# Gate and up as pairs of 64-row matmuls on two row tiles

## The chip, the cores and the metric

The kernel runs on one core of a Trainium2 chip. The metric is the device time of one execution in microseconds. A program that is run again differs by some tenths of a per cent; the three runs of the kernel before lie between 1452.52 and 1454.48 us.

## The reference

The kernel computes one block over 2048 tokens of width 576: a layer norm, a linear attention `s`, a gated feed-forward part, and a product of both.

```python
xn = _layernorm(x)                       # x: 2048 x 576
s = _A_ref(xn, A_wqkv, A_wo)             # linear attention, 32 heads of 18
g = xn @ B_w_gate                        # 576 x 4608
u = xn @ B_w_up                          # 576 x 4608
h = _gelu(g) * u
return x + s * _silu(h @ B_w_down)       # 4608 x 576
```

All operands are fp32. The matrices of gate, up and down are the bulk of the work.

## The kernel before

TensorE works through five stages: `kv` and `q` (projections of the normalized x), `s` (the attention's output, kept in DRAM), gate and up, and down. The change lies in gate and up, with small edits where their operands are formed.

**Words.** A matmul on fp32r operands keeps part of the mantissa. So every operand is split into a high part (a copy by ScalarE that rounds, `act(..., AF.Copy)`) and the remainder (a subtraction by VectorE), and a product is taken in several passes: high by high, high by remainder, remainder by high.

**Seven products for eight.** A gate or up matrix of one group `g` (256 columns of 4608) is multiplied by a scheme of Strassen's kind (`matrix`, from L916): K is split into two halves of 288, the 256 columns into two blocks of 128, and the tokens into blocks of 512. Seven products in place of eight give four output blocks. On the side of the weights GpSimd forms the sums S1 to S4 (`mat_sums`), on the side of x VectorE formed T1 to T4 once (`difference`, L337). The seven products write PSUM banks al, be, ga, de; three of them add to a bank that is begun already:

| product | bank | weights, x |
|---|---|---|
| 0 | al | A11, B11 |
| 1 | be | S2, T2 |
| 2 | ga | S1, T1 |
| 3 | de | S3, T3 |
| 4 | al, added | A12, B21 |
| 5 | ga, added | S4, B22 |
| 6 | de, added | A22, T4 |

Each is done for two sides of the tokens, s = 1 and then s = 0 (tiles named `xo_` and `xr_`, the latter read back from DRAM by `back`). There are 18 groups, gate and up by turns: 36 matrices, `q` from 0 to 35.

**Passes.** A half of K has 288 = 128 + 128 + 32 rows. The operand tiles hold five blocks for it: high parts 0 and 1, a mixed block 2 in which the last 32 rows stand several times as high parts and remainders, and remainders 3 and 4. `product` (L907) runs the seven passes of `PASSES`, each a matmul of 128 rows, 128 columns of weights and 512 tokens.

**What follows a product** is written behind it in `matrix`: copies and sums of the banks by ScalarE and VectorE, gelu and the multiplication in `done`, and the pieces of `todo`: the cutting of the next matrix's weights into words (`mat_pieces`, `cut_w`), the load of the matrix after (`load_mat`), and `run_events`, which issues the sums over h (GpSimd) and their stores to DRAM (SP's queue). The order on every engine is the order of the program. There are six banks for be, ga and de, two of their own for al.

**Down** begins behind matrix 35. `down_first` puts its first loads and cuts into that matrix's `todo`: `load_reg("22")` and `load_reg("42")` (weights of down into the places of B11 and T2 of side 0, `REG` and `X_BACK` both 13 and 7), `load_unit(0, ...)` (tiles `raw_a`, `raw_b` from DRAM) and `cut`. They go through SP's queue, in that order. The bd matmuls need `hi` (ScalarE) and the remainder in `raw_a` (VectorE).

Lines in the profile: L147 is the helper `mm`, L141 `act`, L144 `vec`, L150 `pool`, L153 `dma`; L909 is the matmul in `product`.

## Time and profile before

| | |
|---|---|
| median of three runs | 1453.16 us |
| the profiled execution | 1452.58 us |
| its span on the core | 1450.9 us |
| instructions | 22169 |
| granted clock of TensorE | 1.00 |

The profile is one execution. PE is TensorE's matmuls, PEld its loads of weights, DVE VectorE, ACT ScalarE, POOL GpSimd, SP the engine that issues most DMAs. A group reads: line, engine, operation, names (out<-in), shape, count | busy us, mean ns of one | idle us before, and who ended it. `128*128` is the rows and columns of the array in use. A row of a stretch gives, engine by engine, the busy us with the count in brackets, then the granted clock, the share of the DMA engines and GB/s. A row of the timeline gives start, duration, engine, line, operation, names, shape and count, and in square brackets the idle time before it. A row of waits gives who waited for whom: total us, times, longest.

### The profile page before, as it was taken

What the parts mean: (1) busy time and instruction counts of PE and PEld (TensorE: products, weight loads), DVE (VectorE), ACT (ScalarE), POOL (GpSimd) and SP (SyncE); (2) the same over time, 40 slices, a digit from 0 to 9 for tenths busy, and PEclk for the clock granted to TensorE, in tenths of its full rate; (3) what the DMA queues carried; (4) which work ended last, traced back from release to release, by engine and by line L of the source; (5) the groups of instructions that cost most, each with busy time, mean ns of one, the idle gap of its engine ahead of it and who ended that gap; (6) DMA issues with size and microseconds to landing.
All of it is one profiled execution on the core that took longest, in us unless ns stands there. A gap on an engine that the chain in (4) does not pass through costs nothing.

```text
span 1450.9 us, 22169 instructions
## 1 busy us (share of the span) xinstructions
PE 1444.4 (100%) x8272; PEld 1286.5 (89%) x8272; DVE 1148.7 (79%) x1609; ACT 565.2 (39%) x918; POOL 580.1 (40%) x520
## 2 busy tenths in 40 slices
PE   9999999999999999999999999999999999999998
PEld 8989989988888888888888888888889999999998
DVE  7688666476787887887777878778888978989898
ACT  6444365333222233322332232332235556555454
POOL 3342340225756567566475754667632000000000
PEclk9999999999999999999999999999999999999999
DMA  5554115521532315224242243323379888767886
GB/s 221 186 205 158 45 36 207 224 95 51 171 101 100 131 52 188 88 95 140 72 159 87 97 150 102 117 87 121 126 272 347 269 261 252 249 188 235 278 293 225
DMA packets 119253, 235.04 MB, mean 162 GB/s; under 512 B 11658, under 2 KB 45354, under 8 KB 117226
## 3 DMA queue, kind: packets, MB, share of 16 engines
q1 hardware_dynamic: 116346, 221.37, 45.4%
q0 software_dynamic: 2656, 12.06, 2.2%
q8 instruction: 65, 1.06, 0.3%
q14 instruction: 42, 0.34, 0.1%
q10 hardware_dynamic: 144, 0.20, 0.0%
HBM read 150.96 MB, written 82.58 MB: 161 GB/s over the span
## 4 chain that ended last, share of the span: by engine, by line
PE 97%; DVE 1%; ACT 1%; issue 0%; POOL 0%; DVEq 0%; ACTq 0%; POOLq 0%
PE bd L147 25%; PE al L909 16%; PE ga L909 16%; PE de L909 16%; PE kv L147 8%; PE be L909 8%; PE s L147 4%; PE q L147 3%; PE kv_a L147 1%; PE idle L147 0%; PE d L147 0%; PE kw L147 0%; PE b L147 0%; ACT e_q L141 0%; PE xt L264 0%
## 5 line engine op out<-in xcount | busy, mean ns | idle before, releaser
L150 POOL TENSOR_TENSOR sm<-raw 128x384 f32<-128x384 f32 x72 | 75.0, 1041 | 144.0 <-DMA raw<-in_wgu_dram 125.8
L147 PE MATMUL kv<-wkv,xo_B 128*128 128x412 f32 (+2 forms) x662 | 125.0, 347 | 0.3 <-ACT xo_B L141 0.3
L147 PEld LDWEIGHTS kv<-wkv,xo_B 128*128 128x128 f32 x662 | 120.2, 188 | 1.7 <-ACT xo_B L141 0.9
L144 DVE TENSOR_TENSOR wa<-sm,wa 128x768 fp32r<-128x768 f32 x72 | 90.5, 1257 | 36.0 <-ACT wa L141 35.2
L147 PE MATMUL bd<-w_head,hi 128*128 128x288 f32 x516 | 117.5, 294 | 0.0
L144 DVE TENSOR_TENSOR wb<-raw,wb 128x256 fp32r<-128x256 f32 (+1 forms) x108 | 103.2, 955 | 7.2 <-ACT wb L141 5.5
L144 DVE TENSOR_TENSOR wa<-raw,wa 128x256 fp32r<-128x256 f32 x72 | 66.8, 928 | 50.6 <-ACT wa L141 47.4
L141 ACT ACTIVATE hi<-raw_h 128x1024 fp32r<-128x1024 f32 x59 | 62.5, 1059 | 96.1 <-PE bd L147 55.7
L147 PE MATMUL bd<-w_end,hi 128*128 128x288 f32 x448 | 89.4, 294 | 0.0
L141 ACT ACTIVATE spot_h<-spot_h 128x512 f32<-128x512 f32 x49 | 30.7, 633 | 150.1 <-DVE spot_h L144 150.1
L147 PEld LDWEIGHTS bd<-w_head,hi 128*128 128x128 f32 x516 | 86.8, 188 | 0.1
L144 DVE TENSOR_TENSOR raw_h<-raw_h,hi 128x1024 fp32r<-128x1024 f32 x59 | 71.8, 1221 | 18.8 <-ACT hi L141 18.8
L141 ACT ACTIVATE wa<-sm 128x1152 fp32r<-128x1152 f32 x36 | 41.8, 1161 | 92.8 <-PE de L909 92.8
L147 PE MATMUL bd<-w_end,raw_h 128*128 128x288 f32 x264 | 77.6, 294 | 0.0
L141 ACT ACTIVATE u<-al 128x512 f32<-128x512 f32 x72 | 41.0, 592 | 90.0 <-PE al L909 60.0
L147 PEld LDWEIGHTS bd<-w_end,hi 128*128 128x128 f32 x448 | 71.6, 188 | 0.0
L147 PE MATMUL bd<-beside,raw_h 128*128 128x288 f32 x240 | 70.5, 294 | 0.0
L150 POOL TENSOR_TENSOR spot_h<-spot_h,spot_h 128x512 f32<-128x512 f32 x45 | 62.8, 1403 | 2.9 <-DVE spot_h L144 2.4
L909 PE MATMUL al<-xo_B,wa 128*128 128x512 f32 x252 | 63.0, 389 | 0.0
L909 PE MATMUL al<-xr_B,wa 128*128 128x512 f32 x252 | 63.0, 389 | 0.0
L909 PE MATMUL be<-xo_T,wa 128*128 128x512 f32 x252 | 63.0, 389 | 0.0
L909 PE MATMUL be<-xr_T,wa 128*128 128x512 f32 x252 | 63.0, 389 | 0.0
(278 smaller groups left out, 4036.8 us busy)
## 6 DMA issues: line engine op xcount, KB each, us to landing
raw_h<-hs SPq DMA_DIRECT2D x176, 256.0 KB
raw<-in_wgu_dram SPq DMA_DIRECT2D x36, 768.0 KB
hs<-spot_h SPq DMA_DIRECT2D x90, 256.0 KB
hs<-spot_g SPq DMA_DIRECT2D x80, 256.0 KB
b<-in_wd_dram SPq DMA_DIRECT2D x42, 432.0 KB
hs<-spot_m SPq DMA_DIRECT2D x38, 256.0 KB
raw_g<-hs SPq DMA_DIRECT2D x22, 256.0 KB
raw_a<-hs SPq DMA_DIRECT2D x20, 256.0 KB
```

The lines of the kernel that those rows point to most:

```text
L141: pin(nc.scalar.activation(*args, **kw))
L144: pin(getattr(nc.vector, op)(*args, **kw))
L147: pin(nc.tensor.matmul(*args, **kw))
L150: pin(getattr(nc.gpsimd, op)(*args, **kw))
L909: nc.tensor.matmul(o, w[0:rows, wi, :], xop[0:rows, xi, :], start=(start and n == 0), stop=(n == len(PASSES) - 1), skip_group_check=True,)
```

## The change

The 128-row matmuls of gate and up become pairs of 64-row matmuls. The lower half of the array (rows 0 to 63) works for one side of the tokens while the upper half (rows 64 to 127) works for the other, each into its own bank (`tile_size` 64x128). Since each side needs both halves of K's rows, a product has two phases: in the early one (`phase(False, ...)`) side 1 has the lower and side 0 the upper rows, in the late one (`phase(True, ...)`) the other way. Below, E4 and L4 are the early and the late phase of product 4, and products of the next matrix are counted on (7, 8, ...).

The last 64 rows of K (32 of each half) leave the seven products. They are multiplied apart, as a tail of three more pairs (one early, two late) behind products 3 to 6, with tiles of x that hold their high parts in one half of the rows and the remainders in the other (`tail`, in block 2 of T1, T2 and T3) and with weights cut by `cut_tail`. The weight tiles hold four blocks for each of four matrices and the tail behind them.

`step` orders the work: early phase, a one-column read of the first bank by ScalarE (`seen`), the work that follows the product two before, and then the late phase of the product before. `flush` ends the last one.

```diff
+MAIN = ((0, 0), (0, 2), (2, 0), (1, 1), (1, 3), (3, 1))
+XW = (0, 1, 3, 4)
+TAIL = {"T1": (0,), "T3": (1,), "T2": (0, 1)}
+TR = P // 2
...
     def difference(s, i):
-        vec("tensor_sub", f[o], f[a], f[b])
+        vec("tensor_sub", f[o][:, 0:2], f[a][:, 0:2], f[b][:, 0:2])
...
+    def tail(s, nm, o):
+        h = s * TR
+        for j in range(2):
+            vs = [xf[s][BS[b][j]][:, 2, :] for b in TAIL[nm]]
+            r, low = (slice(i + j * KR, i + (j + 1) * KR) for i in (h, TR - h))
+            v = vs[0][r]
+            if len(vs) == 2:
+                d = tmp([P, TBN], f"xd_{s}_{j}")
+                vec("tensor_sub", d[r], v, vs[1][r])
+                v = d[r]
+            act(o[r], v, AF.Copy)
+            vec("tensor_sub", o[low], v, o[r].bitcast(F32))
...
-        sm = mid(2, [P, 4, 3, P], F32, f"sm_{q}")
+        sm = mid(2, [P, 4, 2, P], F32, f"sm_{q}")
...
     def cut_w(o, src):
-        act(o[:, :, 0:3, :], src, AF.Copy)
-        vec("tensor_sub", o[:, :, 3:5, :], src[:, :, 0:2, :], o[:, :, 0:2, :].bitcast(F32))
-        vec("tensor_sub", o[r, :, 2, :], src[r, :, 2, :], o[r, :, 2, :].bitcast(F32))
+        act(o[:, :, 0:2, :], src, AF.Copy)
+        vec("tensor_sub", o[:, :, 2:4, :], src, o[:, :, 0:2, :].bitcast(F32))
...
-    def product(o, w, xop, start):
-        for n, (wi, xi, rows) in enumerate(PASSES):
-            nc.tensor.matmul(o, w[0:rows, wi, :], xop[0:rows, xi, :], ...)
+    def half_passes(rows, o, w, xop, tail_, late):
+        wi = [(w[rows, i, :], xop[rows, XW[k], :]) for i, k in MAIN]
+        if tail_:
+            wt_, xt_ = tail_
+            wi += [(wt_[rows, i, :], xt_[rows]) for i in range(1 + late)]
+        return [(o, a, b) for a, b in wi]
...
+    def step(prod, post):
+        phase(False, prod)
+        for s in TOUCH:
+            act(seen[:, s : s + 1], prod["o"][s][:, 0:1], AF.Copy)
+        for f in posts[:-1]:
+            f()
+        del posts[:-1]
+        for p in begun_:
+            phase(True, p)
+        begun_[:] = [prod]
+        posts.append(post)
...
+        both("al", "A11", "B11", True, post_0)
+        both("be", "S2", "T2", True, post_1)
+        both("ga", "S1", "T1", True, post_2)
+        both("de", "S3", "T3", True, post_3, tail_of(1, "T3"))
+        both("al", "A12", "B21", False, post_4, tail_of(0, "T1"))
+        both("ga", "S4", "B22", False, post_5, tail_of(0, "T3"))
+        both("de", "A22", "T4", False, post_6, tail_of(1, "T2"))
```

`post_0` to `post_6` hold what stood behind the seven products before, unchanged. The host lays the weights out as four blocks of 128 rows and one in which the last 64 rows stand twice (1280 words a partition for 1536).

Three places in the order. TensorE in matrix 20 (a gate matrix): `de_20_1` is bank de of side 1, `xo_1_T3` its x operand, `wa` a tile of weights. Before, products 2 and 3:

```order
L909 MATMUL ga_20_1_6346<-xo_1_T1_2335,wa_2927 128x512 [waits DVE_49]
L909 MATMUL ga_20_1_6346<-xo_1_T1_2335,wa_2927 128x512 x6
L909 MATMUL ga_20_0_6354<-xr_T1_2885,wa_2927 128x512 [waits DVE_49]
L909 MATMUL ga_20_0_6354<-xr_T1_2885,wa_2927 128x512 x6
L909 MATMUL de_20_1_6367<-xo_1_T3_2469,wa_2927 128x512 [waits DVE_49]
L909 MATMUL de_20_1_6367<-xo_1_T3_2469,wa_2927 128x512 x6
L909 MATMUL de_20_0_6375<-xr_T3_3037,wa_2927 128x512 [waits DVE_49]
L909 MATMUL de_20_0_6375<-xr_T3_3037,wa_2927 128x512 x6
```

And now, the end of E3 (its last pair is the tail) and the start of L2:

```order
L152 MATMUL de_20_1_8371<-xo_1_T3_2485,wa_2952 128x512
L152 MATMUL de_20_0_8372<-xr_T3_3060,wa_2952 128x512
L152 MATMUL de_20_1_8371<-xo_1_T3_2485,wa_2952 128x512
L152 MATMUL de_20_0_8372<-xr_T3_3060,wa_2952 128x512
L152 MATMUL ga_20_0_8335<-xr_T1_2910,wa_2952 128x512 [waits Activation_49]
L152 MATMUL ga_20_1_8334<-xo_1_T1_2348,wa_2952 128x512
L152 MATMUL ga_20_0_8335<-xr_T1_2910,wa_2952 128x512
L152 MATMUL ga_20_1_8334<-xo_1_T1_2348,wa_2952 128x512
```

The two sides alternate matmul by matmul, product 2 ends behind the early phase of product 3, and the late phase waits for ScalarE's one-column read.

ScalarE in the same matrix, around the reads of bank al that end product 4. Before:

```order
L141 ACTIVATE wa_2927<-sm_21_6294 128x3x384 [waits PE_49,Activation_49,Pool_49]
L141 ACTIVATE spot_g2_3060<-al_20_1_6299 128x512 [waits DMAHW7_49,PE_49]
L141 ACTIVATE spot_h2_3055<-al_20_0_6307 128x512 [waits DMAHW3_49,PE_49]
L141 ACTIVATE wb_3036<-raw_21_6244 128x384 [waits Activation_49]
L141 ACTIVATE wb_3036<-raw_21_6244 128x384
```

And now:

```order
L146 ACTIVATE wa_2952<-sm_21_8253 128x3x256 [waits Pool_49]
L146 ACTIVATE eps_t_63<-de_20_0_8372 128x1 [waits PE_49,Activation_49]
L146 ACTIVATE spot_g2_3083<-al_20_1_8258 128x512 [waits DMAHW1_49,Pool_49]
L146 ACTIVATE spot_h2_3078<-al_20_0_8259 128x512 [waits DMAHW5_49,Pool_49]
L146 ACTIVATE wb_3059<-raw_21_8234 128x256 x3
```

The one-column read (`eps_t<-de`, which waits for E6) stands ahead of both reads of al.

TensorE where gate and up end and down begins. Before:

```order
L909 MATMUL de_35_1_8804<-xo_1_T4_2682,wb_3036 128x512 [waits DVE_49]
L909 MATMUL de_35_1_8804<-xo_1_T4_2682,wb_3036 128x512 x6
L909 MATMUL de_35_0_8812<-xr_T4_3051,wb_3036 128x512 [waits DVE_49]
L909 MATMUL de_35_0_8812<-xr_T4_3051,wb_3036 128x512 x6
L147 MATMUL bd_0_0_8922<-w_head0_8830,hi_8858 128x288 [waits DVE_49,Activation_49]
```

And now:

```order
L152 MATMUL de_35_0_12288<-xr_T2_2711,wb_3059 128x512
L152 MATMUL de_35_1_12287<-xo_1_T2_2563,wb_3059 128x512
L152 MATMUL de_35_0_12288<-xr_T2_2711,wb_3059 128x512
L152 MATMUL de_35_1_12287<-xo_1_T2_2563,wb_3059 128x512
L152 MATMUL bd_0_0_12493<-w_head0_12380,hi_12425 128x288 [waits DVE_49,Activation_49]
```

The last pairs of the stage are tails that read T2. On SP's queue the order is as before: `b_22`, `b_42` (into the place of `xr_T2`), and behind it the loads of `raw_a` and `raw_b`.

More of the change, by code (lines that the diff above doesn't have):

```diff
@@ new lines, in phase @@
+    def phase(late, prod):
+        o, w, xs_, start, tails_ = prod["o"], prod["w"], prod["x"], prod["start"], prod["tail"]
+        pair = []
+        for rows, s in ((LOWER, 0 if late else 1), (UPPER, 1 if late else 0)):
+            pair.append([
+                (s, *p) for p in half_passes(rows, o[s], w, xs_[s], tails_ and tails_[s], late)
+            ])
+        n = len(pair[0])
+        for k in range(n):
+            for side in range(2):
+                s, o_, a, b = pair[side][k]
+                mm(
+                    o_, a, b, start=(start and not late and k == 0), stop=(late and k == n - 1),
+                    skip_group_check=True,
+                )
@@ L947, in matrix, with tail_of, both @@
-        both("ga", "S4", "B22", False)
-        for s in SBS:
-            done(s, 0, 1, (u[s], bs["ga", s]))
-        run(todo[5])
-        both("de", "A22", "T4", False)
-        for s in SBS:
-            done(s, 1, 0, (u[s], bs["de", s]))
-        run(todo[6])
+        wtail = wt["tail", q % 2]
+        def tail_of(f, nm):
+            c = slice(f * P, (f + 1) * P)
+            return [(wtail[:, :, c], X[s][nm][:, 2, :]) for s in range(2)]
+        def both(bk, wn, xn, start, post, tail_=None):
+            if start:
+                for s in SBS:
+                    bs[bk, s] = (own_bank if bk == "al" else bank)(f"{bk}_{q}_{s}")
+            step({
+                "o": [bs[bk, s] for s in range(2)], "w": w_at(q, wn), "start": start,
+                "x": [X[s][xn] for s in range(2)], "tail": tail_,
+            }, post)
@@ new lines, in post_4, with post_5, post_6 @@
+        def post_4():
+            for s in SBS:
+                done(s, 0, 0, bs["al", s])
+            run(todo[4])
+        def post_5():
+            for s in SBS:
+                done(s, 0, 1, (u[s], bs["ga", s]))
+            run(todo[5])
+        def post_6():
+            for s in SBS:
+                done(s, 1, 0, (u[s], bs["de", s]))
+            run(todo[6])
+        both("al", "A11", "B11", True, post_0)
+        both("be", "S2", "T2", True, post_1)
+        both("ga", "S1", "T1", True, post_2)
```

142 lines of the change are left out of this document (85 added, 57 removed).

## The prediction, made before the changed kernel ran

> **What bounds the kernel now.** I read the page first, then the busy time by stage, the chain of waits, and the groups of instructions of TensorE with their shapes. The page:
>
> ```profile
> span 1450.9 us, 22169 instructions
> PE 1444.4 (100%) x8272; PEld 1286.5 (89%) x8272; DVE 1148.7 (79%) x1609; ACT 565.2 (39%) x918; POOL 580.1 (40%) x520
> PEclk9999999999999999999999999999999999999999
> PE 97%; DVE 1%; ACT 1%; issue 0%; POOL 0%; DVEq 0%; ACTq 0%; POOLq 0%
> PE bd L147 25%; PE al L909 16%; PE ga L909 16%; PE de L909 16%; PE kv L147 8%; PE be L909 8%; PE s L147 4%; PE q L147 3%; PE kv_a L147 1%; PE idle L147 0%; PE d L147 0%; PE kw L147 0%; PE b L147 0%; ACT e_q L141 0%; PE xt L264 0%
> ```
>
> The chain is TensorE for 97%, and L909, the gate and up products, is 56% of it. The stages (two halves of gate and up, then down):
>
> ```profile
> core 0: us, PE busy (x) PEld busy (x) DVE busy (x) ACT busy (x) POOL busy (x), PEclk, DMA share, GB/s
> 276.33:676.20 399.87, 399.87 (x1766) 331.09 (x1765) 306.08 (x410) 118.07 (x194) 230.17 (x185) 1.00 0.34 118
> 676.20:1076.05 399.85, 399.85 (x1765) 331.08 (x1764) 313.50 (x415) 117.13 (x190) 244.44 (x197) 1.00 0.35 120
> 1076.05:1446.50 370.45, 370.27 (x2809) 369.72 (x2807) 331.71 (x384) 194.63 (x237) 20.07 (x26) 1.00 0.82 265
> ```
>
> TensorE has no hole in gate and up. The stage lasts 399.87 + 399.85 = 799.7 us for 36 matrices of 98 matmuls, so 226.7 ns each, at a granted clock of 1.00. Nothing done by other engines can shorten it; only fewer or denser matmuls can. Three pieces of the chain give the pitch by width:
>
> ```profile
> 505.02 3.17 PE ga L909 x14
> 1076.22 156.68 PE bd L147 x1190
> ```
>
> 512 columns take 3.17 / 14 = 226 ns, 288 columns 156.68 / 1190 = 131.7 ns. The line through both has (226.7 - 131.7) / 224 = 0.424 ns a column and 9.6 ns that do not depend on width: each matmul carries a gap of about 10 ns.
>
> **The change: slots.** A matrix had 7 products x 2 sides x 7 passes = 98 full matmuls. Now it has 7 products x 2 phases x 6 pairs = 84, and 4 tails of 1 + 2 pairs = 12: 96 pairs. If a pair takes what a full matmul took, 36 x 2 x 226.7 ns = **16.3 us** go. Whether it does is the first open price: no row shows two row tiles. The nearest rows are column tiles, d (32 columns each) beside full transposes of the same 128x128 shape and type:
>
> ```profile
> 196.82 1.30 PE L147 MATMUL d<-ph,small 128*32 128x128 f32 x40
> L147 PE MATMUL d<-ph,small 128*32 128x128 f32 x160 | 5.2, 275 | 0.0
> 22.63 0.82 PE L264 MATMUL xt<-ident,x 128*128 128x128 f32 x6
> L264 PE MATMUL xt<-ident,x 128*128 128x128 f32 x24 | 3.4, 276 | 0.0
> ```
>
> Forty d matmuls start (1300 - 275) / 39 = 26 ns apart, six transposes (820 - 276) / 5 = 109 ns apart: four column tiles run side by side, weight loads included. I take the same for two row tiles. The load of weights:
>
> ```profile
> L909 PE MATMUL al<-xr_B,wa 128*128 128x512 f32 x252 | 63.0, 389 | 0.0
> L909 PEld LDWEIGHTS al<-xr_B,wa 128*128 128x128 f32 x252 | 47.3, 188 | 9.8
> ```
>
> A load takes 188 of the 226.7 ns and lies under the matmul before it. A pair needs two. Side by side, they still take 188 and stay hidden. One after the other at the closest spacing that a row shows for such loads, 131.7 ns (one for each bd matmul), they take 263 ns and bind. Above nothing, the gap of 10 ns could vanish under the other tile's stream: 512 x 0.424 = 217 ns. So a pair lies between 217 and 263 ns; I take 226.7, since the d rows show no change of pitch by tiling beyond the sharing.
>
> The Trainium skill ("TensorE: Matmul & The Clock Gate", Back-to-back issue gap) gives 512 columns an isolated gap of N / 2.4 + 2.5, so 216 ns; the row says 226.7, so the trace disagrees here, and by the page the pairs would come to 3456 x 216 = 746 us.
>
> "Every operand at a multiple of 256 bytes" I cost at nothing: weight blocks are 128 words and token blocks 512 words in the tiles of both versions.
>
> **Order and waits in gate and up.** Early and late phases interleave (E5 L4 E6 L5 E7), each followed by work two products late. An early phase is 6 or 7 pairs, a late one 6 or 8. The tightest chain is bank al: product 4 ends with L4, product 7 (the next matrix) opens with E7. Between them lay 28 matmuls, 6.3 us; now E6 and L5, 7 + 8 pairs, 3.4 us. And ScalarE's reads of al stand behind the one-column read that waits for E6. Rows for ScalarE:
>
> ```profile
> 633.38 1.75 PE L909 MATMUL al<-xr_B,wa 128*128 128x512 f32 x7
> 633.58 0.60 ACT L141 ACTIVATE u<-al 128x512 f32<-128x512 f32 x1 [4.15 <-PE al L909]
> L141 ACT ACTIVATE st<-st 128x1 f32<-128x1 f32 x4 | 0.8, 203 | 0.1
> L141 ACT ACTIVATE spot_h<-al 128x512 f32<-128x512 f32 x23 | 13.4, 589 | 3.4 <-PE al L909 3.4
> L141 ACT ACTIVATE wb<-raw 128x384 fp32r<-128x384 f32 x36 | 16.8, 517 | 0.0
> ```
>
> The last al matmul of the first side started one pitch before 633.38, so ScalarE follows 0.43 us after a start. From the start of E6's last matmul in a gate matrix: 0.43 + 0.20 (one column) + 2 x 0.59 = 1.8 us. E7 is due at 9 x 0.227 = 2.0 us. It holds, by 0.2 us. In an up matrix VectorE reads al, not behind that wait, and has more room.
>
> The next chain is VectorE's. Behind al, ScalarE cuts the new weights, VectorE takes three 256-word remainders and only then the sums that free ga and de:
>
> ```profile
> L144 DVE TENSOR_TENSOR wb<-raw,wb 128x256 fp32r<-128x256 f32 x36 | 41.4, 1151 | 0.9
> L144 DVE TENSOR_TENSOR spot_g<-u,ga 128x512 f32<-128x512 f32 x30 | 20.4, 683 | 3.7 <-PE ga L909 3.7
> DVE spot_h L144 <- DMA hs<-spot_h: 13.5, 6, 2.4
> ```
>
> From L5's start: 1.9 us to the first remainder (1.8, less a pitch, and 0.35 for its first half), 3 x 1.15, 2 x 0.68: ga is free at 6.7 us and E9 is due at 34 pairs, 7.7 us. For de: one more remainder and two more sums end at about 8.6 to 9; E10 is due at 46 pairs, 10.4 us. The six waits on a spot's DMA, 13.5 / 6 = 2.25 us each, which had cover, can now reach TensorE by 0.5 to 1.5 us: 3 to 9 us. Against that VectorE loses its four 32-row subtractions a matrix. I take **+3 us** for all of this, 0 to 12.
>
> What VectorE loses and the smaller loads of weights (five blocks of K instead of six) are worth nothing by themselves, since TensorE covers them.
>
> **Before the stage.** The sums T are formed on two thirds of the words, and the last 64 rows go their own way. For the first 1024 tokens VectorE gains eight 32-row subtractions and loses three there (the fourth is later), and a third of three sums:
>
> ```profile
> L144 DVE TENSOR_TENSOR xf_B<-xf_B,xf_B 128x1536 f32<-128x1536 f32 x3 | 6.4, 2127 | 0.1
> L144 DVE TENSOR_TENSOR xo_T<-xf_B,xo_T 32x512 fp32r<-32x512 f32 x3 | 3.0, 1009 | 0.1
> 80.00:115.00 35.00, 34.69 (x198) 29.68 (x198) 31.69 (x53) 18.56 (x32) 13.07 (x11) 1.00 0.49 186
> ```
>
> That is 5 x 1.0 - 2.1 = +2.9 us on an engine with 3.3 us free between 80 and 115 us. **+1 us**, 0 to 3.
>
> **The end of the stage.** The last products now read T2 (tile xr_T2) in their tail, as the very last pairs of gate and up. In the kernel before, its last reader was product 1 of the last matrix. The register load b_42 of the down phase goes into that place, stands on SP's queue ahead of the eight loads raw_a and raw_b, and waits for that reader. So all of them now start when gate and up are over. Before:
>
> ```profile
> 1057.21 3.55 SPq L153 DMA_DIRECT2D b<-in_wd_dram  x2
> 1066.78 1.76 SPq L153 DMA_DIRECT2D raw_a<-hs  x4
> 1063.08 1.41 ACT L141 ACTIVATE w_head<-b 128x1440 fp32r<-128x1440 f32 x1 [2.96 <-DMA b<-in_wd_dram]
> 1070.22 1.06 ACT L141 ACTIVATE hi<-raw_a 128x1024 fp32r<-128x1024 f32 x1 [4.69 <-DMA raw_a<-hs]
> 1072.11 1.22 DVE L144 TENSOR_TENSOR raw_a<-raw_a,hi 128x1024 fp32r<-128x1024 f32 x1
> 1062.00:1066.00 4.00, 4.00 (x19) 3.33 (x18) 2.17 (x4) 2.46 (x2) 0.00 (x0) 1.00 1.06 380
> ```
>
> A load b of 1.3 MB took 1063.08 - 1057.21 = 5.9 us; the first two raw_a took 1070.22 - 1066.78 = 3.4 us, or 0.52 MB / 380 GB/s = 1.4 us if they queue behind b. From the end of gate and up: 0.4 (matmul's end) + 5.9 + 1.4 + 1.06 + 1.22 = 10 us until the third bd matmul can go; if raw_a overtakes b, 0.4 + 0.4 + 3.4 + 2.3 = 6.5 us. Nothing covers it: TensorE has no other work. **+9 us**, 6 to 10.
>
> **Sum**, against the profiled run's 1452.6 us (span 1450.9), 0.6 us under the median of the runs: 1452.6 - 16.3 + 3 + 1 + 9 = 1449.3, about **1449.5 us** on the scale of the median. A measurement of this kernel can tell about 0.2% from no change, 2.9 us; the forecast is 3.7 us down.
>
> **Rivals.**
>
> *The gap goes* (faster). With two tiles in turn, one tile's gap lies under the other's stream. For: the column tiles' weight loads do overlap; against: the d rows' pitch is no less than one shared stream. 3456 x 217.1 = 750.3 us, 49.4 us less; with +13: 1452.6 - 49.4 + 13 = 1416 us.
>
> *Banks come back late* (slower). E7 waits for al behind ScalarE's one-column wait. The ledger's 0.2 us is gone if ScalarE is still cutting weights when E6 ends, or a spot's DMA holds the read. At 0.8 us for each of 36 matrices, 29 us: 1449.5 + 29 = 1478 us. It decides from 0.1 us a matrix on, 3.6 us in all. For: the way is half as long as before; against: ScalarE is busy 30% of the stage.
>
> *Loads one behind the other* (slower). 263.4 ns a pair: 3456 x 263.4 = 910.3 us, +110.6: 1452.6 + 110.6 + 13 = 1576 us. The change loses from 228 ns a pair on, since 13 us of costs stand against 16.3. For: 188 ns twice does not fit in 226.7; against: the d rows.
>
> *No load under its own tile's matmul* (slower). Each tile would load, then stream: 188 + 226.7 = 415 ns a pair, 1434 us, so 2100 us. Against it the full tiles: the load groups are busy 331 of 400 us while TensorE never stops. The Trainium skill ("TensorE: Matmul & The Clock Gate", The mechanism) says that a load overlaps matmuls in flight only when its row group differs; the rows of the full tiles disagree.
>
> **How the numbers follow.** Forecast 0.45, the gap goes 0.22, banks late 0.13, loads in a row 0.17, no overlap 0.03. The range holds the first three, 0.80: from 1416 less the front and mid-stage costs and some pitch, 1402, to banks late with 4 us more, 1482. The forecast's own range, with its unknown costs at both ends, is 1442 to 1461. Of its 0.45 I give 0.25 to faster by over 0.2%, 0.17 to within, 0.03 to slower. With the rivals: faster 0.47, same 0.18, slower 0.35.
>
> **What would show it.** In the profile after: the pitch of a pair in the chain's pieces (226.7 ns, or 217, or 263); idle time of TensorE before al named ScalarE; a hole of 6 to 10 us at the first bd, released through raw_a. A pair far from 226.7 ns, or no hole at bd, proves me wrong.

## The result: 1.6% slower

The changed kernel takes 1476.19 us (median of 4 runs, 1474.18 to 1477.23) against 1452.84 us before (4 runs, 1452.39 to 1454.48): a ratio of 1.0157, 95% interval 1.0139 to 1.0175. The forecast was 1449.5 us, 3.7 us faster. The profiled execution took 1477.23 us. Its page:

```profile
span 1475.4 us, 29114 instructions
PE 1441.6 (98%) x11656; PEld 1299.7 (88%) x11656; DVE 993.8 (67%) x1491; ACT 574.5 (39%) x1217; POOL 515.5 (35%) x520
PEclk9999999999999999999999999999989999999999
PE 85%; DVE 6%; DMA 5%; ACT 2%; issue 1%; POOL 1%; SPq 0%; ACTq 0%; DVEq 0%; POOLq 0%
```

TensorE is still busy 98% of the span, which tells nothing: what changed is the chain. TensorE held 97% of it before and holds 85% now; VectorE, DMA and ScalarE have 13%. The row of the clock has an 8, where it had none. Gate and up in two halves, the turn to the down stage, and the down stage (columns as in the rows of before):

```profile
287.40:686.90 399.50, 394.70 (x3470) 343.42 (x3471) 226.05 (x350) 120.62 (x340) 199.35 (x185) 1.00 0.33 112
686.90:1086.45 399.55, 393.92 (x3447) 326.64 (x3443) 230.63 (x344) 116.30 (x328) 212.57 (x197) 1.00 0.31 105
1086.45:1095.07 8.62, 0.38 (x3) 0.00 (x0) 1.38 (x2) 2.22 (x2) 0.00 (x0) 0.69 0.86 300
1095.07:1471.00 375.93, 373.35 (x2808) 371.84 (x2808) 336.73 (x389) 196.31 (x239) 20.70 (x26) 0.99 0.82 264
```

Gate and up issue fewer slots and last as long as before, now with 10 us in which TensorE stands. The third row is new: 8.6 us between the last pair and the first bd, with the clock at 0.69. The longest of TensorE's waits (us in total, times, longest):

```profile
PE bd L152 <- ACT hi L146: 8.2, 1, 8.2
PE kv L152 <- ACT xo_B L146: 4.8, 1, 4.8
PE de L152 <- DVE spot_h L149: 3.5, 6, 0.9
PE ga L152 <- DVE spot_m L149: 3.2, 1, 3.2
PE al L152 <- DMA xr_B<-kept_B: 1.7, 1, 1.7
PE bd L152 <- DVE raw_h L149: 1.7, 3, 1.2
```

The wait on spot_h stands with those on spot_g (1.4 us) and spot_m (0.5 us) in one family: eight holes of 0.3 to 1.4 us before a de, one in every four matrices from 405 us on, 5.4 us together. From start to start these eight places cost 7.5 us: the record of a matmul lasts 0.39 us, 0.16 longer than its pitch, and hides that much of each wait, and the next pair comes 0.11 us later still.

By the first and last start of each stage's matmuls, in us:

| | to the first s | s stage | gate and up | last de to first bd | down | span |
|---|---|---|---|---|---|---|
| before | 209.24 | 67.09 | 799.50 | 0.23 | 370.30 | 1450.87 |
| changed | 215.53 | 71.88 | 799.05 | 8.62 | 375.86 | 1475.41 |
| difference | +6.29 | +4.79 | -0.45 | +8.39 | +5.56 | +24.54 |

Some 4.5 us behind the last bd are not in the columns, before and after alike. The difference of the spans is the difference to be explained. The pair itself is as forecast; two pieces of the chain near the end of gate and up, 7 and 8 pairs:

```profile
1081.62 1.59 PE de L152 x14
1083.21 1.81 PE ga L152 x16
```

1.59 / 7 and 1.81 / 8 are 227 and 226 ns a pair. 3455 pitches of 226.7 ns are 783.3 us; the stage's 799.05 us are 15.8 us more, and that is where the gain of the slots went inside the stage.

Three rows show the clock, two at the hole before kv and one behind the first bd:

```profile
114.00:120.00 6.00, 1.18 (x7) 0.86 (x6) 5.38 (x12) 3.91 (x7) 2.50 (x2) 0.74 0.44 110
120.00:124.00 4.00, 4.00 (x13) 3.81 (x14) 1.70 (x6) 2.54 (x7) 1.48 (x2) 0.54 0.94 303
...
1096.00:1100.00 4.00, 3.67 (x15) 3.67 (x16) 3.93 (x7) 1.42 (x2) 0.76 (x2) 0.51 1.06 395
```

From 120 to 124 us TensorE is busy all the time, with 13 matmuls at a clock of 0.54; the stage's usual clock is 1.00. A hole may so cost twice: its own time, and the slow matmuls behind it. In the record of the clock the granted share is 0.50 four times before the last bd, for 6.83, 3.41, 3.41 and 10.24 us, all multiples of 3.41 us: from 116.88, 250.00, 1055.54 and 1089.68 us on.

A theory from these rows: the pairs give their 16.3 us, and waits at a few places, each with a cause of its own (forming T2's tail, stores behind a load, sums of the last weights, the places of T2 at the end), take some 41 us (24.5 + 16.3) with the half clock behind them. Rival: the pairs leave other engines too little time throughout, so that any cure only moves the wait on. The runs undo one place at a time, then all. Ten of the kernels measured here, the changed one among them, have the same front, and in their profiled executions the first s starts between 214.83 and 218.23 us (215.53 in the changed kernel); so a place behind the front is judged by its own stage's length, not by times from the start.

### The profile page after: what moved, and what is told of

Read it like the earlier page. It is cut to its first block, busy times and chain, and to the rows that moved or that the text cites. A ratio compares the mean times of both kernels' runs of the same rounds, so it can differ in the third digit from the quotient of the medians.

```text
span 1475.4 us, 29114 instructions
## 1 busy us (share of the span) xinstructions
PE 1441.6 (98%) x11656; PEld 1299.7 (88%) x11656; DVE 993.8 (67%) x1491; ACT 574.5 (39%) x1217; POOL 515.5 (35%) x520
## 3 DMA queue, kind: packets, MB, share of 16 engines
q8 instruction: 92, 1.51, 0.4%
## 4 chain that ended last, share of the span: by engine, by line
PE 85%; DVE 6%; DMA 5%; ACT 2%; issue 1%; POOL 1%; SPq 0%; ACTq 0%; DVEq 0%; POOLq 0%
PE bd L152 23%; PE de L152 15%; PE al L152 13%; PE ga L152 13%; PE kv L152 8%; PE be L152 5%; PE s L152 3%; DMA hs<-spot_h 2%; PE q L152 2%; DVE wb L149 1%; PE kv_a L152 1%; DVE xo_T L149 1%; DMA xr_B<-kept_B 1%; DVE raw_h L149 0%; DVE sx L149 0%
## 5 line engine op out<-in xcount | busy, mean ns | idle before, releaser
L152 PE MATMUL de<-xr_T,wa 64*128 64x512 f32 x540 | 140.7, 388 | 5.4 <-DVE spot_h L149 3.5
L152 PE MATMUL de<-xo_T,wa 64*128 64x512 f32 x540 | 141.9, 388 | 0.0
L152 PE MATMUL de<-xo_T,wb 64*128 64x512 f32 x540 | 139.7, 386 | 0.0
L152 PE MATMUL de<-xr_T,wb 64*128 64x512 f32 x540 | 139.7, 386 | 0.0
L152 PE MATMUL ga<-xr_T,wa 64*128 64x512 f32 x486 | 127.7, 387 | 0.0
L152 PE MATMUL ga<-xo_T,wa 64*128 64x512 f32 x486 | 127.7, 387 | 0.0
L152 PE MATMUL ga<-xo_B,wb 64*128 64x512 f32 x432 | 110.1, 387 | 3.2 <-DVE spot_m L149 3.2
L152 PE MATMUL al<-xr_B,wb 64*128 64x512 f32 x432 | 110.6, 389 | 1.7 <-DMA xr_B<-kept_B 1.7
L152 PE MATMUL al<-xo_B,wb 64*128 64x512 f32 x432 | 110.6, 389 | 0.0
L152 PE MATMUL ga<-xr_B,wb 64*128 64x512 f32 x432 | 110.0, 388 | 0.1
```

The costliest lines, as they stand in the source:

```text
L152: pin(nc.tensor.matmul(*args, **kw))
```

## The experiments

### The end of the stage: b_42 alone (e1_b42_later)

```
         [lambda: load_reg("22", "22")],
-        [lambda: load_reg("42", "42")],
+        [],
...
         [lambda: load_reg("32", "32"), lambda: cut(1)],
-        [],
+        [lambda: load_reg("42", "42")],
```

> Only the register load b_42 moves on SP's queue, from ahead of the raw_a and raw_b loads to behind them. Theory of the prediction (b_42 alone holds the end of the stage): the hole of 8.2 us before the first bd goes, TensorE has nothing over 1 us there, the time falls from 1476.2 by 8.2 us and by another 2 us of half clock, to about 1466. Rival (a second instruction waits for the same last pairs: w_end, which goes into the place of xo_T2, started at 1086.87, the moment they ended, and ScalarE's first hi stands behind it): the hole shrinks only to w_end 1.2 + hi 1.1 = about 2.3 to 3 us and the time to about 1470.

1470.68 us (4 runs), ratio 1.0119 (1.0104 to 1.0134). The rival was right: 2.2 us of hole stay before the first bd and 1.05 us before the third. ScalarE in this run:

```profile
1087.34 1.16 ACT L146 ACTIVATE w_end<-b 128x1152 fp32r<-128x1152 f32 x1 [3.39 <-PE de L152]
1088.41 1.99 ACT L146 ACTIVATE hi<-raw_a 128x1024 fp32r<-128x1024 f32 x2
```

w_end waits for the last pairs (the de named in brackets), since it goes into the place of xo_T2, and the first hi stands behind it. T2's tail is read last on both sides of the tokens, so it holds two places: the one that the prediction named, and a second one that it did not.

### Both places (e2_b42_wend_later)

Against the run before:

```
-                lambda: make_words(0, 1), lambda: cut(0),
+                lambda: cut(0),
...
-            [lambda: load_reg("42", "42")],
+            [lambda: load_reg("42", "42"), lambda: make_words(0, 1)],
```

> As the run before, and the second half of product 1's weights (w_end, ScalarE and VectorE) moves behind the first two cuts of raw as well. If the two places of T2 are the whole cause: no hole over 1 us at the first bd, no half clock after it, 1476.2 - 8.2 - 2.4 = about 1465. If the loads themselves are what is late (raw_b waits for xo_T3, read until 3 us before the end): a hole of 2 to 4 us stays, at the fifth matmul block, released through raw_b.

1472.03 us, ratio 1.0129 (1.0114 to 1.0144): no better than with one place. The first bd starts 0.3 us behind the last de, and then TensorE waits 1.6 us at 1093 and 3.7 us at 1102 us, so down takes 379.9 us. The long wait in the chain, and the DMA rows of this run:

```profile
1093.72 11.23 DMA raw_a<-hs
```
```profile
1079.00:1086.00 7.00, 7.00 (x63) 6.72 (x59) 6.30 (x8) 3.56 (x5) 1.87 (x2) 1.00 0.50 173
1086.00:1107.00 21.00, 15.67 (x111) 14.79 (x110) 13.21 (x13) 4.98 (x5) 12.39 (x15) 0.98 1.02 368
```

raw_a for product 2 takes 11.2 us, because the DMA engines are full (share 1.02, 368 GB/s) with two b of 1.3 MB that stand ahead of it. In the changed kernel the same 7 us before the end ran at a share of 0.09. So, by these rows, the place of T2 costs DMA time, not only a wait: what is not loaded under gate and up is paid in the next stage. The next run tests that.

### Other places and another order at the end (e9_end_replaced)

```
-    REG = {"22": 13, "42": 7, "32": 9, ...
+    REG = {"22": 13, "42": 9, "32": 7, ...
...
     LOADS = {
+        0: ("32", "32"),
...
+                lambda: load_reg("42", "42"), lambda: cut(0),
                 lambda: load_unit(0, 2), lambda: load_unit(0, 3), lambda: load_unit(0, 4),
...
+            [lambda: make_words(0, 1)],
```

> The end alone: b_42 takes the place that xo_T1 leaves (free some 6 us before the end of gate and up) and is issued behind the first raw_a; b_32, wanted only in product 4, takes the place of xr_T2 and comes in thirds through product 1; w_end stands behind the two first cuts. Theory (after the two runs in which the hole moved to later loads: the DMA engines idle at 0.09 from 1080 to 1087 us and then have 2.6 MB of b ahead of the raw of product 2): no hole over 1 us at the first bd nor behind it, down at 370 to 372 us, the time 1476.2 - 8.4 - 4 = about 1464. Rival (the places of raw_b and wa come too late in any order): 3 to 5 us of holes stay in product 1 and 2, time 1468 to 1472.

1466.90 us, ratio 1.0085 (1.0071 to 1.0098). The hole before the first bd is gone, 1.6 us before a bd 7 us later stay, and down takes 373.25 us:

```profile
1079.50:1086.50 7.00, 7.00 (x64) 5.99 (x64) 6.31 (x9) 3.57 (x5) 1.86 (x2) 1.00 0.88 295
```

The DMA engines work again under the last pairs (0.88 against 0.09). From the last de to the last bd the changed kernel takes 384.5 us, this one 373.6: 10.9 us. Seven other runs that leave the end alone (e4 to e8, e11, e14) take 381.6 to 383.1 us there, so 8 to 9.5 us are the order's and the rest is chance in the changed kernel's profiled execution. By the medians, 9.3 us, this is the largest of the four places.

### What the clock costs (e3_fill_hole, e3b_fill_33)

```
     flush()
+    fill(70)        # e3b: 33; small matmuls of ident into the first bank of bd
     down_all()
```

> The hole of 8.2 us before the first bd is filled with 70 small matmuls (109 ns each, 7.6 us) that compute nothing needed, everything else as in the changed kernel. If the fall of the granted clock to 0.5 behind the hole costs time of its own: the clock stays at 1.0 there, the first 48 bd take 6.3 us and not 8.2, and the time falls by 2 to 2.5 us, to about 1474, though the hole as such stays. If the clock costs nothing (the first bd wait for data anyway): 1476.

1478.71 us, ratio 1.0177 (1.0159 to 1.0196). I had mis-sized the fill: each counts twice, 140 matmuls took 15.9 us and delayed the first bd to 1101.1 us. Still the time rose by only 2.5 us, since down then took 371.6 us in place of 375.9; but a bd that starts later also finds more of its loads done. With a fill that fits:

> The fill of the hole before the first bd again, with 33 in place of 70 (one counts as two matmuls of 114 ns, so 7.5 us). The first bd starts within 0.5 us of where it does in the changed kernel, measured from the last de. If the fall of the granted clock costs time of its own: down from the first bd to the last takes 373 to 374 us in place of 375.9, and the time is about 1474. If not: 375.9 and 1476.

1475.02 us (1472.44 to 1475.92), ratio 1.0147 (1.0132 to 1.0162). A row of this run, behind the hole:

```profile
1096.00:1100.00 4.00, 3.48 (x25) 3.24 (x25) 3.93 (x7) 2.88 (x3) 0.92 (x2) 1.00 1.07 395
```

Useless work keeps the clock at 1.00 (0.51 in the changed kernel at the same time), and 25 matmuls start from 1096 to 1100 us in place of 15. From the first real bd (1094.9 us) to the last, down takes 373.1 us, the length that I expected, 2.8 us less. But the clock is not the reason. The first 11 us of down, in the changed kernel and in this run:

```profile
1095.07:1106.07 11.00, 10.56 (x61) 9.98 (x62) 10.87 (x13) 4.75 (x5) 5.94 (x8) 0.78 1.00 355
1094.90:1105.90 11.00, 8.92 (x61) 8.21 (x62) 10.86 (x13) 4.63 (x5) 5.93 (x8) 1.00 0.99 345
```

Both have come to the 61st matmul. At the full clock TensorE is ahead for some us and then waits for raw_a and raw_b (0.72, 0.36 and 0.99 us) while the DMA engines are full. So here the half clock lay under a wait for loads and cost nothing. The 2.8 us arise far behind: 600 matmuls on, both stand 82.0 us behind the first bd, and the changed kernel then waits for 1.18 us at 1255 us and for 0.4 us twice near 1465 us, mostly for raw_h. Its 375.9 us are the longest of eight runs with this end, all with a half clock at the turn; the other seven (e4 to e8, e11, e14) take 373.4 to 374.5 us. The medians are 1.2 us apart and their runs overlap.

Where the half clock does cost time is the s stage. The ten kernels that form T2's tail as the changed one does have the same three holes there (1.0, 0.2 and 0.6 us within 3.6 us). In six of them, the changed kernel among them, the clock then falls for 3.41 us, and the stage takes 71.86 to 71.93 us; in four (e3, e3b, e6, e9) it does not, and the stage takes 70.37 to 70.38 us. That is 1.5 us for the half clock alone.

### T2's tail in front (e4_t2_tail_on_pool, e7_t2_tail_all_pool, e11_t2_other_order)

VectorE and ScalarE in the changed kernel, by the chain:

```profile
98.43 0.69 DVE xd L149
99.14 0.64 ACT xo_T L146
99.81 0.68 DVE xo_T L149
100.52 0.69 DVE xd L149
...
101.89 0.61 ACT e_q L146
```

A subtraction, its rounding on ScalarE, the remainder, and the same for the second 32 rows: each engine waits for the other, and e_q, which starts the next group of q, stands on ScalarE behind it. It ran at 97.41 us before and runs at 101.89 us now. First only the subtractions were moved:

```
-                vec("tensor_sub", d[r], v, vs[1][r])
+                sub("tensor_sub", d[r], v, vs[1][r])     # GpSimd for T2
...
-            vec("tensor_sub", o[low], v, o[r].bitcast(F32))
+            sub("tensor_sub", o[low], v, o[r].bitcast(F32))
```

> The four subtractions that form the tail of T2 move from VectorE to GpSimd, for both halves of the tokens. If VectorE's chain through them makes the two holes (4.8 us before kv at 115 us, 1.8 us in the s stage at 247 us, half clock behind both): VectorE gets 4.1 us back at 98 us, the first hole shrinks to under 1 us, the s stage begins 5 to 6 us earlier against the changed kernel, the s stage loses its 1.8 us, and the time falls by 7 to 10 us, to 1466 to 1469. If the hole comes of the other added work (tails of T1 and T3, waits on ScalarE's rounding) or of the queue order: it falls by under 3 us.

1474.86 us, ratio 1.0150 (1.0135 to 1.0165). A miss: the hole before kv is 5.1 us, no smaller, though VectorE is free of T2. The rounding copies on ScalarE now wait for GpSimd, which takes longer:

```profile
98.73 0.63 ACT L146 ACTIVATE xo_T<-xd 32x512 fp32r<-32x512 f32 x1 [3.62 <-POOL xd L155]
102.10 0.63 ACT L146 ACTIVATE xo_T<-xd 32x512 fp32r<-32x512 f32 x1 [2.73 <-POOL xd L155]
102.75 0.60 ACT L146 ACTIVATE e_q<-q 128x512 f32<-128x512 f32 x1
```

In the s stage the same move took 2.6 us off, of which 1.5 us are the half clock that this run did not meet there. In front, by these rows, it was not VectorE that blocked but ScalarE's queue. Then the copies as well:

```
-            act(o[r], v, AF.Copy)
+            if nm == "T2":
+                pool("tensor_copy", o[r], v)
+            else:
+                act(o[r], v, AF.Copy)
```

> All six operations of T2's tail go to GpSimd, the two rounding copies too, so that neither VectorE nor ScalarE has any of them. Theory (after the run that moved only the subtractions and left the hole of 5 us): the copies stand in ScalarE's queue ahead of the e_q activations and wait for the subtractions; with them gone ScalarE's e_q at 102 us comes at 97 to 98 us, the hole before kv at 115 us falls under 1 us, the clock stays at 1.0, the s stage begins about 6 us earlier, and the time is 1476.2 - 6 - 3 = about 1467. Rival (the tails of T1 and T3 and their four copies are as guilty, or GpSimd's own queue then holds the sums ph): 2 to 4 us of the hole stay.

1469.62 us, ratio 1.0114 (1.0097 to 1.0131). e_q is back at 97.75 us, the first s starts 2.1 us earlier and the s stage is 3.65 us shorter (2.2 us against the four runs without half clock in it). But 3.06 us of the hole stay, as the rival had it. The four subtractions that cut one tile of tokens to xo_B, in the changed kernel:

```profile
106.53 1.51 DVE L149 TENSOR_TENSOR xo_B<-xf_B,xo_B 128x256 fp32r<-128x256 f32 x4
```

and the same four in this run, with GpSimd's work at that time (it has none at 106.53 us in the changed kernel):

```profile
102.92 4.68 DVE L149 TENSOR_TENSOR xo_B<-xf_B,xo_B 128x256 fp32r<-128x256 f32 x4
```
```profile
102.61 0.60 POOL L155 CAST xo_T<-xd 32x512 fp32r<-32x512 f32 x1
103.30 1.35 POOL L155 TENSOR_TENSOR xo_T<-xd,xo_T 32x512 fp32r<-32x512 f32 x1
104.73 2.72 POOL L155 TENSOR_TENSOR ph<-ph,e_q 128x512 f32<-128x512 f32 x2
```

Beside GpSimd they take 4.68 us in place of 1.51. The Trainium skill ("SBUF — State Buffer", Summary: rules for kernel authors) says that a VectorE operation with two inputs in SBUF and a GpSimd operation that reads SBUF do not share: the second to issue waits until the first has ended. The trace agrees: 3.2 us more on VectorE, beside 4.7 us of GpSimd's work. So what GpSimd takes off VectorE, it partly takes back. That this is what leaves the hole at 3.06 us is not shown: the next run has nearly the same hole without it.

Last, the same six operations on their first engines in another order (both subtractions of T2 first, then T3's work, the two copies, the two remainders; in the tail of the second half of the tokens, formed in the s stage, the two subtractions, the two copies, the two remainders):

```
+        t2 = tail_steps(0, "T2", last[:, 1])
+        run(t2[0:2])
         act(hi, f[:, 0:2], AF.Copy)
         vec("tensor_sub", lo, f[:, 0:2], hi.bitcast(F32))
+        tail(0, nm, last[:, 0])
+        run(t2[2:])
```

> T2's tail stays on VectorE and ScalarE with the same six operations, but its two subtractions come ahead of the rest of T3's work and the two copies stand together, so that no engine waits for the other. If the waits back and forth (two of 0.7 us on VectorE, and 1.9 us that ScalarE's e_q loses) make the hole before kv: it falls from 4.8 to about 2 to 3 us and the time by 2 to 4 us, 1473. If it is the plain length of VectorE's added work (4 x 0.68 for T2, 2 x 0.68 for T1 and T3): it falls by under 1.5 us, 1475.

1471.97 us, ratio 1.0123 (1.0108 to 1.0139): 4.2 us off for an order alone. The hole is 3.07 us, the first s 1.5 us earlier, the s stage 2.8 us shorter, 1.5 of them the half clock that does not fall there now.

### Stores ahead of the weights (e5_stores_first)

SP's queue in the changed kernel, and the store in the chain:

```profile
399.33 0.33 SPq L158 DMA_DIRECT2D raw<-in_wgu_dram  x1
399.76 0.38 SPq L158 DMA_DIRECT2D hs<-spot_h  x1
```
```profile
399.76 5.31 DMA hs<-spot_h
...
405.09 0.70 DVE spot_h L149
```

The load of the next weights waits for VectorE's last remainder, a store of a spot stands behind it, goes out with 0.65 MB ahead of it, takes 5.3 us, and VectorE's sum into the same place waits for it; TensorE then waits for the bank. (In the kernel before, the same store took as long: it was issued at 390.06 us and released VectorE at 395.73 us.)

```
-        todo[4].append(lambda q=q: load_mat(q + 2))
         for i in range(7):
             todo[i].append(lambda at=7 * q + i: run_events(at))
+        todo[4].append(lambda q=q: load_mat(q + 2))
```

> The stores of a spot go out on SP's queue ahead of the load of the weights two matrices on, not behind it. If the eight holes of 0.3 to 1.4 us before de (5.4 us in all) come of stores that run behind that load's 0.65 MB: the stores of that place take about 2.3 us and not 5.3, the eight holes fall under 0.2 us each, and the time falls by about 5 us, to 1471. If VectorE is simply late there (three remainders ahead of its sums): the holes stay within 1 us in sum and the time is 1476. The weights load later by under 1 us either way; the hole of 3.2 us at 1051 stays or grows.

1468.19 us, ratio 1.0102 (1.0087 to 1.0117): 8.0 us less, more than expected. All eight holes are gone; gate and up take 790.6 us in place of 799.05, of which the eight places were 7.5. SP's queue now:

```profile
393.94 0.32 SPq L158 DMA_DIRECT2D hs<-spot_h  x1
395.90 0.32 SPq L158 DMA_DIRECT2D hs<-spot_g  x1
399.33 0.33 SPq L158 DMA_DIRECT2D raw<-in_wgu_dram  x1
```

Two stores that were ready go out 4 to 6 us earlier, and the load not a moment later.

### Sums of the next weights later (e6_sums_later)

```
-        mat_sums(q + 1)
+        go = mat_sums(q + 1)
         todo = mat_pieces(q + 1)
+        todo[0].append(go)
```

> GpSimd's four sums of the next weights, which wait for their load, move from ahead of the loop's body into the work behind product 1, so behind the additions of the matrix before. If the hole of 3.2 us at 1051 (and half clock behind it, 0.9 us) comes of additions queued behind sums that wait for a load: it goes, 1476.2 - 4 = 1472. If the last additions are late in themselves (GpSimd has more of them there than time): it stays over 2 us, 1476. Risk: the sums come too late for ScalarE's cut behind product 4, with holes before the next matrix's be.

1484.03 us, ratio 1.0213 (1.0198 to 1.0228): a miss, 7.8 us slower. The hole at 1051 us shrinks from 3.2 to 1.7 us, but the eight holes before de grow to 1.4 to 2.4 us each. VectorE's three remainders of the weights and the load that waits for them, in this run:

```profile
398.12 3.88 DVE L149 TENSOR_TENSOR wb<-raw,wb 128x256 fp32r<-128x256 f32 x3 [1.67 <-ACT wb L146]
```
```profile
402.03 0.33 SPq L158 DMA_DIRECT2D raw<-in_wgu_dram  x1
```

They took 2.64 us in the changed kernel, with the load at 399.33 us. GpSimd's additions, now later, run on beside them; that this is what stretches them is argued from e7's rows, not tried by itself. In the runs below only the last sums are moved.

### Is it the row tiles? (e8_sides_apart, e14_one_row_tile)

```
-        for k in range(n):
-            for side in range(2):
+        for side in range(2):
+            for k in range(n):
```

> The same matmuls as in the changed kernel, but within a phase the 6 to 8 of the lower row tile all stand ahead of those of the upper one; they do not alternate. If two row tiles run side by side only where their matmuls stand next to each other in the queue: all but the ends of a phase run singly at 226.7 ns, gate and up take between 6912 x 226.7 x 6/7 = 1343 and 1567 us in place of 799, and the time is 2020 to 2240. If TensorE looks past the matmuls in front: no change, 1476.

1512.95 us (one run). The first of the two expectations was wrong by some 500 us; the second, no change, is nearer. Gate and up take 837.5 us, 5% more, though up to 7 matmuls of the same row tile stand between the two that now run side by side:

```profile
501.26 0.39 PE L152 MATMUL al<-xo_B,wa 64*128 64x512 f32 x1
501.43 0.39 PE L152 MATMUL ga<-xo_T,wa 64*128 64x512 f32 x1
501.49 0.39 PE L152 MATMUL al<-xo_B,wa 64*128 64x512 f32 x1
501.66 0.39 PE L152 MATMUL ga<-xo_T,wa 64*128 64x512 f32 x1
```

The matmuls of al and of ga, of two phases, run interleaved, each at its own pitch of 220 to 240 ns. In the changed kernel the two of a pair start within 30 ns.

```
-        for rows, s in ((LOWER, 0 if late else 1), (UPPER, 1 if late else 0)):
+        for rows, s in ((LOWER, 0 if late else 1), (LOWER, 1 if late else 0)):
```

> Both matmuls of each pair read the lower 64 rows, so both stand on one row tile and the upper half of every product's K is left out (the lower counts twice); all sizes and counts stay. If two row tiles are what makes a pair as short as one matmul: each of the 6912 takes 226.7 ns by itself, gate and up take 1567 us, and the time is about 1476 + 770 = 2245, less what the longer stage hides, 2225 to 2245. If a matmul of 64 rows is short in itself: under 1800.

2244.12 us (one run), as expected:

```profile
288.23:1855.10 1566.87, 1566.87 (x6913) 1271.73 (x6912) 438.32 (x693) 233.72 (x668) 400.60 (x382) 1.00 0.16 55
```

6912 matmuls take 1566.9 us, 226.7 ns each. So, on one row tile, a matmul of 64 rows costs as much as one of 128, and that the pairs stand on two row tiles is all that makes them short.

### The cures together (e10_all, e12_all_2, e13_all_2_front_pool)

e10 joins e9, e5, e7, the sums of the last matrix behind product 1, and the loads of B21 and B22 ahead of the second weights.

> The end as in the run beside it, stores first, the tail of T2 on GpSimd, the sums of the last matrix behind the additions, and the loads of B21 and B22 ahead of the second weights. If the losses are separate and add: 1476.2 - 12 (end) - 8 (stores) - 6.6 (tail) - 4 (sums) - 1.7 (loads) = 1444, 0.6% under the kernel before. If they share their time (the engine that waits is late again behind the next wait): 1450 to 1456, no faster than the kernel before.

1452.72 us (11 runs), ratio 0.9994 (0.9985 to 1.0003): as fast as the kernel before. The parts did not add up: a new hole of 2.6 us stood in the first matrix (the second weights took 11.7 us to load behind what was put ahead of them, and ScalarE's cut waits for them), 1.75 us at 1038 us, 1.6 us behind the first bd. The second version takes these three up (the edits against the changed kernel):

```
-    load_mat(1)
-    back("B21", "B22", "T4", eng=nc.sync)
+    back("B21", eng=nc.sync)
+    load_mat(1)
+    back("B22", "T4", eng=nc.sync)
...
+        if q == NQ - 2:
+            todo[1].append(go)
+        else:
+            go()
...
+        posts[0]()
+        make_words(0, 1)
+        cut(2)
+        posts[1]()
```

> The cures together, second version: of the loads after the s stage B21 goes ahead of the second weights and B22 behind; the last sums stand behind product 2; the last weights and the third cut of raw stand ahead of the last closing sums; and for the first 1024 tokens the subtractions of T2 come first on VectorE, its last ones on GpSimd. If the gain of the slots is real and only waits hide it: the hole of 2.6 us in the first matrix, of 1.75 us at 1038 and of 1.6 us behind the first bd go, and the time is 1452.7 - 5 = 1447 to 1448, 0.4% under the kernel before. If new waits take their place: 1451 to 1455.

> As the run beside it, but T2's tail of the first 1024 tokens wholly on GpSimd. The run e7 and the run e11 left the same hole of 3.06 us before kv. If VectorE's work sets it and the mix in the run beside takes 1.4 us off VectorE: this one has a hole of 3.1 us, the run beside 1.5 to 2. If VectorE slows while GpSimd runs (in e7 a subtraction of 281 ns took 1.26 us beside GpSimd), both have about 3 us and the same time.

e12 takes 1449.30 us (10 runs), ratio 0.9972 (0.9962 to 0.9981); e13, which differs in the front alone, 1448.25 us (4 runs), ratio 0.9964 (0.9950 to 0.9978). Both beat the kernel before by some 0.3%. e12's gate and up, and down:

```profile
283.86:1069.87 786.01, 785.15 (x6914) 671.32 (x6913) 455.19 (x696) 239.53 (x670) 412.39 (x382) 1.00 0.32 113
1069.87:1442.30 372.43, 371.05 (x2809) 369.97 (x2808) 336.48 (x388) 196.83 (x239) 21.65 (x26) 1.00 0.83 268
```

Gate and up lose 0.9 us to holes (786.01 less 785.15 busy). The hole before kv is 3.48 us in e12 and 3.07 us in e13: neither mix takes it away. e7, e10 and e13 issue the same instructions up to the first s, and their holes are 3.06, 3.07 and 3.07 us. What differs is the clock behind the hole: it is halved for 3.41 us, not at all, and for 6.83 us, and the first s starts at 213.46, 212.22 and 214.52 us. So the half clock costs 1.2 and 2.3 us there.

| | to the first s | s stage | gate and up | last de to first bd | down | span |
|---|---|---|---|---|---|---|
| e12 less before | +5.84 | +1.69 | -13.80 | +0.09 | +2.10 | -3.49 |

The last 0.6 us to the span's end lie behind the last bd.

## Why the prediction was wrong

The profiled execution was forecast at 1449.3 us and took 27.9 us more: 12.8 in gate and up, 10.1 before it and 5.0 at the end. All three were priced too low, in part for steps that were left out.

**The slots: right.** A pair was put at 226.7 ns out of 217 to 263, and takes 226.7; e14 shows that two row tiles are the reason, and e12 that 13.8 of the 16.3 us come out of the stage once its waits are cured. So the rivals "the gap goes", "loads one behind the other" and "no load under its own tile's matmul" are refuted.

**The end of the stage: size of the hole right, step half right.** +9 was forecast, +8.4 came. But b_42 was named as what holds the end, and e1 shows w_end behind it in the same way, e2 the DMA time behind both. And "TensorE has no other work" priced the hole alone: down itself takes 5.6 us longer. 3.0 of these are lost by the 61st matmul (10.9 us behind the first, 7.9 before) to the late loads; e3b loses as much at the full clock. The other 2.5 are later waits, mostly on raw_h, and seven runs with the same end lose 1.3 to 2.5 us less in down: this part is largely chance.

**Before the stage: wrong, by 10 us.** The step that failed is "5 x 1.0 - 2.1 = +2.9 us on an engine with 3.3 us free between 80 and 115 us", taken as +1 us. +6.3 us came before the s stage. VectorE was not short of time: it was busy for 29.52 of those 35 us, against 31.69 before. T2's tail is a chain that goes twice from VectorE to ScalarE and back, and what it held was ScalarE's e_q (e4 against e7). The 6.3 us are about the hole (4.8 us, 0.3 before) and 2.0 us of half clock behind it. The second half of the tokens was left out altogether: its tails are formed in the s stage, and that lost another 4.8 us, 1.5 of them by the half clock; e7 gives back 3.65, with these 1.5. The order of the same operations alone is worth 4.2 us in all (e11).

**Order and waits in gate and up: wrong size.** +3 was forecast, 0 to 12; 15.8 us came. The named danger, bank al behind ScalarE's one-column read, cost nothing: no wait of TensorE names it. The spot's DMA was named too, with "3 to 9 us", and then taken with all the rest at +3. Its eight places are 7.5 us, and e5 gives back 8.5 us of the stage. The 2.25 us of the row before were what was left of a wait; the store itself, behind the weights' load, took as long before, and VectorE's wait for it grew only to 16.5 / 6 = 2.75 us. What went is the cover. Not in the sum at all were the additions behind GpSimd's sums of the last matrix (a wait of 3.2 us, 4.1 from start to start, and 1.4 us of half clock behind it) and the loads after the s stage, wanted 10.1 us behind the first al by the new order, and 14.3 us before (2.0 us from start to start).

**The half clock: no term.** Each of the larger waits left TensorE at half its clock for some microseconds; in the kernel before the profile shows this nowhere. Half of TensorE's busy time at the low clock is 2.0 us before the s stage, 1.7 in it, 1.7 at 1056 us and 2.2 at the first bd. The last of these cost nothing (e3b); the s stage's is 1.5 us by the runs, so some 5 us of the 24.5 are the half clock's.

The sum on the profiled runs, with the measured terms: 1452.6 - 16.3 + 15.8 (gate and up) + 6.3 + 4.8 (before) + 8.4 + 5.6 (the end) = 1477.2, as it must be, since the terms are read from the same execution. The rival "banks come back late" gives 1478 and so almost the right time, for a reason that did not occur: that is luck.

Of the rival theory, that any cure moves the wait on, this much is true: e2, e6 and e10 did so, each by a new order of loads or sums. e12 ends it: with 3.5 us of hole left in front, the change is a small gain. The front's +5.8 us in e12 are about this hole and the half clock behind it: 6.83 us of it, and half of TensorE's busy time in them is 2.8 us. What keeps a hole of 3 us or more there in e7 and e10 to e13 stays open.

## What to carry to other kernels

When a stage is packed denser, list what its last operand's place, its queues and its neighbours' orders hold back, and price the next stage's loads, not only the first wait. Idle time of an engine that waits in a chain is no room for more work; cost an added step with every engine that it goes through, and with what stands in those queues behind it. A hole in TensorE's work can cost more than its length, in slow matmuls behind it: 0, 1.2 and 2.3 us behind the same hole of 3.1 us in three runs, nothing where the next loads were late anyway. And one profiled execution can hold some microseconds of chance; a term read from it is safer when several runs that leave its stage alone agree.

## What the runs showed of the hardware that I had not expected

- The two row tiles run side by side even with up to 7 matmuls of one tile between theirs in the queue: 837.5 us against 799.05 in e8. How far TensorE can look was not tried.
- The clock fell behind a single hole of 4.8 us, 3.2 us and 8.2 us. Behind smaller ones it fell in some runs and not in others: behind the s stage's three holes of 1.0, 0.2 and 0.6 us in six of ten, behind one of 1.5 to 1.9 us near 298 us in three of eleven (e3, e4, e6), and behind one of 3.06 us before kv in e7 and e13 and not in e10:

```profile
118.00:124.00 6.00, 6.00 (x32) 5.97 (x33) 4.57 (x11) 2.93 (x7) 1.50 (x2) 1.00 0.91 305
```
```profile
118.00:124.00 6.00, 6.00 (x18) 5.73 (x19) 2.62 (x8) 2.82 (x7) 1.47 (x2) 0.52 0.96 327
```

  The first row is e10's, the second e13's: 32 matmuls against 18 in the same 6 us. The Trainium skill ("TensorE: Matmul & The Clock Gate", Part 1: The HAM clock gate) has a window of 3.4 us that runs freely, and half the clock after one idle window. That holes of one length fare differently, and that the half clock lasts multiples of 3.41 us, agrees with such a window. That the window must be idle does not agree: the s stage's three small holes, with TensorE busy between them, and a single one of 1.74 us (e3) still brought the clock down.
- GpSimd beside VectorE: 1.51 us of VectorE's subtractions became 4.68 us (e7).
